# Channel groups with one block's and with three blocks' kernels by turns in block 0, each kind with its own tile of finished rows

## The chip, the cores and the metric

The kernel runs on one core of a Trainium2 chip. The metric is the device time of one execution in microseconds (us). Three runs of the kernel before took 1357.64, 1360.15 and 1365.32 us, median 1360.15.

## The reference

A state-space convolution (S4D) and a feed-forward layer, each behind a layer norm with modulation, on 2048 tokens of 576 channels, all in float32:

```
K  = 2 * Re(sum_n C[d,n] * exp(A[d,n]*dt[d]*l))        # 576 convolution kernels, 2048 long, 128 states
mod = silu(c) @ w_mod                                  # sa, ca, ga, sb, cb, gb
h = layernorm(x) * (1 + ca) + sa
x = x + ga * (causal_conv(h, K) + h * D_skip)          # by FFT of 4096
h = layernorm(x) * (1 + cb) + sb
x = x + gb * (relu(h @ w1) @ w2)                       # 576 -> 4608 -> 576
```

## The kernel before

The tokens are worked through in four blocks of 512. The convolution is done block by block with transforms of its own; block s needs the convolution kernel's rows for block s (called kd[s] in DRAM, in two halves of the channels, p = 0 and 1). The 576 channels are dealt with in 12 groups h of 48; groups 0 to 5 make half p = 0, groups 6 to 11 half p = 1.

A start stage (up to about 222 us) makes the tables W1 and W2 of every group, the rows of block 0, and the convolution of block 0. From then on the feed-forward layer of block b runs as a loop over 36 tiles of the hidden size. Each such step has 14 matmuls into hps (line 1309), ScalarE's relu hh (line 1314), VectorE's remainder hl (line 1315), and 14 matmuls into acc (line 1335) one step later, in TensorE's order. In block 0 a step also splits its weights into a high and a low part (lines 1274 to 1291) and stores the low part for the later blocks.

Between these steps the function `step` takes pieces from a generator of side work, at four places in each step; it stops when the pieces' VectorE estimates or the number of TensorE pieces reach its bounds. The side work of block 0 is `kg.rest`, which makes the kernel rows of blocks 1 to 3, and then the convolution of block 1. A scheduler then sets the order on each engine from its own estimates, so instructions stand somewhat moved against the code.

`kg.rest` goes through a plan of groups. Each entry says for which blocks the group makes rows: `(1, 2, 3)` for groups 0 to 5, a heavy group, and `(1,)` for groups 6 to 11, a light one (blocks 2 and 3 of those follow in block 1's side work). For each group it loads W1 and Z (`load0`) and W2 (`load2`, 1536 KB) on GpSimd's queue, turns W1 on VectorE once for each block (`rot`, lines 464 to 470), and then makes the products on TensorE (line 498) in two halves: 48 channels' matmuls of 48 columns in a heavy group, of 16 in a light one, copied by ScalarE into the tile `ker` (line 508). When half of the channels is done (h % 6 == 5), the rows are stored to kd on SyncE's queue (line 432). Products of one group are mixed with the rotations of the next:

```python
yield from spread(rots(h, W1, W0, Z), prev, len(plan[h]))
prev = products(h, W1, W2)
```

`spread` gives one piece of products after every `len(plan[h])` pieces of rotations, so the products of the group before are spread over 12 pieces of a heavy group's rotations, or over 4 of a light one's. W1 has two buffers, W2 two, the tile `ker` one, and the PSUM tile kps one. The convolution of block 1 begins behind the plan's end: it loads the rows as kt (line 1232, GpSimd's queue) and transforms them (ps_f, line 829).

Of the kernel before, what the change touches and what calls it, by code (L numbers as in the profile page):

```python
# [10 lines left out]
F32 = mybir.dt.float32  # L11
F32R = mybir.dt.float32r
I32 = mybir.dt.int32
AF = mybir.ActivationFunctionType
# [4 lines left out]
P = 128  # L19
L = 2048  # L20
D = 576
# [7 lines left out]
NH = 12  # L29
# [20 lines left out]
class KGen:  # L50
# [10 lines left out]
    def v(self, out, a, b, op):  # L61
        self.tc.keep_in_program_order(self.nc.vector.tensor_tensor(out, a, b, op=op))  # L62
# [373 lines left out]
    def rest(self, psum, plan):  # L436

        nc, k = self.nc, self.k
        v = nc.vector.tensor_tensor
        hs = list(plan)  # L440
        with ExitStack() as ctx:
            pt = k.pool(ctx, f"kr{len(hs)}", side="right")
            most = used = 16 * max(len(b) for b in plan.values())

            d = Kept(k.tc, nc.gpsimd).dma_start

            def load0(h):
                W0 = pt.tile([P, 16, 2, H], F32, tag="W0", bufs=3, name=f"W0_{h}")
                Z = pt.tile([P, 2, 2, H], F32, tag="Z", bufs=3, name=f"Zr_{h}")
                d(out=W0.rearrange("p a r c -> p (a r c)"), in_=k.W1d[h])  # L450
                d(out=Z.rearrange("p i r c -> p (i r c)"), in_=k.Zd[h])
                return W0, Z

            def load2(h):
                W2 = pt.tile([P, 2, 32, H], F32, tag="W2", bufs=2, name=f"W2r_{h}")
                d(out=W2.rearrange("p r b c -> p (r b c)"), in_=k.W2d[h])
                return W2

            def rot(out, X, Z, i):
# [4 lines left out]
                v(T.rearrange(flat), X.rearrange(flat), zi, op=ALU.mult)  # L464
                yield 1.75
                v(out.rearrange(flat), X.rearrange(flat), zr, op=ALU.mult)  # L466
                yield 1.75
                v(out[:, :, 0], out[:, :, 0], T[:, :, 1], op=ALU.subtract)
                yield 0.95
                v(out[:, :, 1], out[:, :, 1], T[:, :, 0], op=ALU.add)  # L470
                yield 0.95

            def rots(h, W1, W0, Z):
                blocks = plan[h]
                a = [W1[:, 16 * i : 16 * i + 16] for i in range(len(blocks))]
                if blocks[0] == 1:
                    yield from rot(a[0], W0, Z, 0)
                    if len(blocks) > 1:
                        yield from rot(a[1], W0, Z, 1)
                        yield from rot(a[2], a[0], Z, 1)  # L480
                else:
                    yield from rot(a[0], W0, Z, 1)
                    yield from rot(a[1], a[0], Z, 0)

            ke = [None]

            def products(h, W1, W2):
                blocks = plan[h]
                na = 16 * len(blocks)
                if h % 6 == 0:  # L490
                    ke[0] = pt.tile([P, most, 72], F32, tag="ke", bufs=1, name=f"ker_{h}")[:, :na]
                for half in range(2):
                    ps = psum.tile([P, 6, na], F32, tag="cps", bufs=1, name="kps")
                    for q in range(6):
                        for dd in range(4):
                            ch = dd * 12 + 6 * half + q
                            for r in range(2):
                                nc.tensor.matmul(  # L498
                                    ps[32 * dd : 32 * dd + 32, q, :],
                                    W2[:, r, :, ch],  # L500
                                    W1[:, :, r, ch],
                                    start=(r == 0),
                                    stop=(r == 1),
                                )
# [3 lines left out]
                    nc.scalar.activation(  # L508
                        ke[0][:, :, q0 : q0 + 6], ps.rearrange("p q a -> p a q"), AF.Copy
                    )  # L510
                    yield None
                if h % 6 == 5:
                    yield -1
                    for i, s in enumerate(blocks):
                        self.store(
                            s, h // 6, ke[0][:, 16 * i : 16 * i + 16].rearrange("p a q -> p (a q)"),
                            nc.sync,
                        )

            nxt = [load0(hs[0])]  # L520
            W2 = load2(hs[0])
            nxt.append(load0(hs[1]))
            yield -1
            prev = iter(())
            for i, h in enumerate(hs):
                W0, Z = nxt.pop(0)
                if i + 2 < len(hs):
                    nxt.append(load0(hs[i + 2]))
                na = 16 * len(plan[h])
                if used + na > most:  # L530
                    all1 = pt.tile([P, most, 2, H], F32, tag="W1", bufs=2, name=f"W1r_{h}")
                    used = 0
                W1 = all1[:, used : used + na]
                used += na
                yield from spread(rots(h, W1, W0, Z), prev, len(plan[h]))
                prev = products(h, W1, W2)
                if i + 1 < len(hs):
                    W2 = load2(hs[i + 1])
            yield from prev


def spread(a, b, n):

    for i, w in enumerate(a):
        yield w
        if i % n == n - 1:
            yield next(b, 0.0)
    yield from b


class Body:
# [3 lines left out]
    def build(self):  # L555
        nc, tc, I = self.nc, self.tc, self.I
        with ExitStack() as ctx:
            dr = ctx.enter_context(tc.tile_pool(name="dram", bufs=1, space=DRAM))
            self.kd = [[dr.tile([P, 16 * 72], F32, name=f"kd_{s}_{p}") for p in range(2)] for s in range(NB)]
            self.W2d = [dr.tile([P, 64 * H], F32, name=f"W2d_{h}") for h in range(NH)]  # L560
            self.W1d = [dr.tile([P, 32 * H], F32, name=f"W1d_{h}") for h in range(NH)]
            self.Zd = [dr.tile([P, 4 * H], F32, name=f"Zd_{h}") for h in range(NH)]
            spec = lambda n, m: [
                [dr.tile([P, 8 * PC], F32, name=f"{n}_{i}_{p}") for p in range(2)] for i in range(m)
            ]
            self.Ud, self.Rd = spec("Ud", 4), spec("Rd", 3)
            self.Kd = self.Rd[:1] + spec("Kd", 3)[1:]
            self.md = {n: dr.tile([1, D], F32, name=f"md_{n}") for n in ("ca", "sa", "gb")}
            self.cst = ctx.enter_context(tc.tile_pool(name="cst", bufs=1))
            self.L1d = [dr.tile([P, 640], F32, name=f"L1d_{f}") for f in range(NF)]  # L570
            self.L2d = [dr.tile([P, D], F32, name=f"L2d_{f}") for f in range(NF)]
            self.consts()
            self.x2, self.xT, self.ended = {}, {}, -1
            self.dsk = self.cst.tile([1, D], F32, name="dsk")
            nc.gpsimd.dma_start(out=self.dsk, in_=I["dsk"].unsqueeze(0))
            self.sm = self.pool(ctx, "sm")
# [168 lines left out]

    def main(self, ctx, kg, hooks):
        nc, tc, I = self.nc, self.tc, self.I
        for n, w in (("sb", 5), ("cb", 5), ("gb", D)):
# [790 lines left out]
```

## Time and profile before

| | us |
|---|---|
| median of 3 runs | 1360.15 (1357.64 to 1365.32) |
| the profiled execution | 1357.89 |
| its span, first to last instruction | 1356.1 |
| TensorE busy | 1239.6 (91%) |
| VectorE busy | 891.6 (66%) |
| ScalarE busy | 494.9 (36%) |
| GpSimd busy | 162.6 (12%) |
| mean granted TensorE clock | 0.944 of full speed |

PE is TensorE, PEld its weight loads, DVE VectorE, ACT ScalarE, POOL GpSimd, SP SyncE. A row of a group has the line, engine, operation, tiles and count, then busy time and the mean of one in ns, then the engine's idle time just ahead and what ended it. A row of the busy times by stretches has, behind the stretch's length, each engine's busy time, then the granted TensorE clock, the mean busy share of the DMA engines and GB/s. "issue" is time in which an engine waited for nothing that the profile shows. The feed-forward loop of block 0 runs from about 222 to 569 us.

### The profile page before, as it was taken

What the parts mean: (1) busy time and instruction counts of PE and PEld (TensorE: products, weight loads), DVE (VectorE), ACT (ScalarE), POOL (GpSimd) and SP (SyncE); (2) the same over time, 40 slices, a digit from 0 to 9 for tenths busy, and PEclk for the clock granted to TensorE, in tenths of its full rate; (3) what the DMA queues carried; (4) which work ended last, traced back from release to release, by engine and by line L of the source; (5) the groups of instructions that cost most, each with busy time, mean ns of one, the idle gap of its engine ahead of it and who ended that gap; (6) DMA issues with size and microseconds to landing.
All of it is one profiled execution on the core that took longest, in us unless ns stands there. A gap on an engine that the chain in (4) does not pass through costs nothing.

```text
span 1356.1 us, 26019 instructions
## 1 busy us (share of the span) xinstructions
PE 1239.6 (91%) x10720; PEld 986.5 (73%) x10720; DVE 891.6 (66%) x1324; ACT 494.9 (36%) x863; POOL 162.6 (12%) x260
## 2 busy tenths in 40 slices
PE   4566777899989999999999999999999999999997
PEld 2345555677767687777777887887888888888885
DVE  5889988999955899678556986367997222111112
ACT  5678423222122432622234225433322353233231
POOL 0657511000010100020000000100000000000000
PEclk9558887999978999999999999999999999999998
DMA  8557973776897877798778995777996557666651
GB/s 267 221 223 291 328 271 130 282 249 248 320 332 277 296 248 269 239 382 311 250 246 327 363 371 158 269 230 245 370 387 194 176 175 228 201 195 195 201 184 53
DMA packets 120843, 345.85 MB, mean 255 GB/s; under 512 B 23916, under 2 KB 24212, under 8 KB 109972
## 3 DMA queue, kind: packets, MB, share of 16 engines
q1 hardware_dynamic: 103828, 226.96, 49.7%
q0 software_dynamic: 16384, 115.85, 22.8%
q8 instruction: 84, 1.38, 0.4%
q10 hardware_dynamic: 512, 1.38, 0.3%
q14 instruction: 35, 0.29, 0.1%
HBM read 262.73 MB, written 81.40 MB: 254 GB/s over the span
## 4 chain that ended last, share of the span: by engine, by line
PE 73%; DVE 15%; DMA 5%; issue 4%; ACT 1%; POOL 1%; SPq 0%; ACTq 0%; DVEq 0%; POOLq 0%
PE acc L1335 29%; PE hps L1309 29%; PE kps L498 4%; PE ps_f L829 4%; PE kps L71 2%; PE ph L71 2%; PE ps_i L1036 2%; DVE T L464 1%; DVE W1r L466 1%; DVE T L62 1%; DMA Ua<-Ud 1%; DVE Y L1015 1%; DMA r<-in_w_dram 1%; DMA kd<-ker 1%; DVE W L62 1%
## 5 line engine op out<-in xcount | busy, mean ns | idle before, releaser
L1309 PE MATMUL hps<-xh,w 128*128 128x512 f32 x1152 | 391.3, 400 | 0.7 <-ACT xh L47 0.7
L1335 PE MATMUL acc<-w,hh 128*128 128x512 f32 x1152 | 371.8, 403 | 7.0 <-ACT hh L1314 7.0
L1315 DVE SCALAR_TENSOR_TENSOR hl<-hps,hh 128x512 fp32r<-128x512 f32 x144 | 99.0, 687 | 322.9 <-ACT hh L1314 321.9
L1335 PEld LDWEIGHTS acc<-w,hh 128*128 128x128 f32 x1152 | 217.6, 190 | 55.1 <-ACT hh L1314 8.3
L1309 PEld LDWEIGHTS hps<-xh,w 128*128 128x128 f32 x1152 | 217.3, 190 | 48.5 <-ACT xh L47 1.3
L1309 PE MATMUL hps<-xl,w 128*128 128x512 f32 x576 | 230.7, 401 | 0.2
L1335 PE MATMUL acc<-w,hl 128*128 128x512 f32 x576 | 224.4, 402 | 3.9 <-DVE hl L1315 3.9
L1314 ACT ACTIVATE hh<-hps 128x512 fp32r<-128x512 f32 x144 | 85.9, 597 | 304.0 <-PE hps L1309 302.3
L1284 ACT ACTIVATE w<-r 128x576 fp32r<-128x576 f32 x141 | 96.6, 685 | 236.7 <-PE acc L1335 207.9
L1335 PEld LDWEIGHTS acc<-w,hl 128*128 128x128 f32 x576 | 109.1, 190 | 28.2 <-DVE hl L1315 5.0
L1309 PEld LDWEIGHTS hps<-xl,w 128*128 128x128 f32 x576 | 108.7, 189 | 24.5 <-DVE xl L47 0.8
L1274 ACT ACTIVATE w<-r 128x640 fp32r<-128x640 f32 x140 | 102.6, 733 | 40.6 <-DMA r<-in_w_dram 40.6
L1309 PE MATMUL hps<-xs,w 128*128 128x512 f32 x288 | 97.1, 410 | 0.3 <-DVE w L1279 0.3
L498 PEld LDWEIGHTS kps<-W1r,W2r 128*32 128x32 f32 x3456 | 66.9, 146 | 32.0 <-issue 23.6
L498 PE MATMUL kps<-W1r,W2r 128*32 128x48 f32 (+2 forms) x3456 | 75.9, 238 | 9.2 <-issue 8.2
L71 PE MATMUL kps<-W,W 128*32 128x16 f32 x2304 | 45.1, 218 | 42.7 <-POOL W L68 28.7
L71 PEld LDWEIGHTS kps<-W,W 128*32 128x32 f32 x2304 | 40.4, 150 | 55.0 <-POOL W L68 30.7
L1015 DVE TENSOR_TENSOR Y<-Y,T 128x1152 f32<-128x1152 f32 x60 | 79.4, 1349 | 0.0
L830 ACT ACTIVATE Z<-ps_f 128x288 f32<-128x288 f32 x120 | 48.7, 408 | 68.8 <-PE ps_f L829 67.6
L1453 POOL DMA_DIRECT2D out_dram<-x x16 | 8.7, 544 | 469.0 <-DVE x L1445 466.3
L1309 PEld LDWEIGHTS hps<-xs,w 128*128 128x128 f32 x288 | 53.3, 188 | 12.4 <-DVE w L1279 0.7
L1335 PE MATMUL acc<-hl,w 128*128 128x512 f32 x144 | 57.3, 398 | 0.0
(230 smaller groups left out, 1567.3 us busy)
## 6 DMA issues: line engine op xcount, KB each, us to landing
r<-in_w_dram SPq DMA_DIRECT2D x144, 320.0 KB, 3.5
r<-in_w_dram SPq DMA_DIRECT2D x144, 288.0 KB, 3.7
w<-L1d SPq DMA_DIRECT2D x108, 320.0 KB
w<-L2d SPq DMA_DIRECT2D x108, 288.0 KB, 2.6
W2r<-W2d POOLq DMA_DIRECT2D x18, 1536.0 KB, 8.3
W2d<-W SPq DMA_DIRECT2D x12, 1536.0 KB, 8.6
Ua<-Ud POOLq DMA_DIRECT2D x15, 1152.0 KB, 9.4
W<-W1d POOLq DMA_DIRECT2D x18, 768.0 KB, 10.7
```

The costliest lines, as they stand in the source:

```text
L62: self.tc.keep_in_program_order(self.nc.vector.tensor_tensor(out, a, b, op=op))
L71: self.tc.keep_in_program_order(self.nc.tensor.matmul(*args, **kw))
L498: nc.tensor.matmul(ps[32 * dd : 32 * dd + 32, q, :], W2[:, r, :, ch], W1[:, :, r, ch], start=(r == 0), stop=(r == 1),)
L829: nc.tensor.matmul(o, fc[:, n2, c, :], src(n2), start=True, stop=True)
L830: ev = nc.scalar.activation(Z[:, n2, c], ps[:, :PC], AF.Copy)
L1015: v(y, y, T, op=op or ALU.add)
L1274: copy(g - 1)(w1[g][:, 0], r1[g], AF.Copy)
L1284: copy(g)(w[:, 0:D], r2[g], AF.Copy)
L1309: nc.tensor.matmul(ps, a, x, start=(i == 0), stop=(i == 13))
L1314: nc.scalar.activation(hh, ps, AF.Relu)
L1315: nc.vector.scalar_tensor_tensor(hl, ps, 0.0, hh, op0=ALU.max, op1=ALU.subtract)
L1335: nc.tensor.matmul(acc[i], a, x, start=(f == 0 and seen[i] == 1), stop=(f == NF - 1 and seen[i] == (3 if i < 4 else 2)),)
```

## The change

The plan of block 0 is no longer in the order of the groups: light and heavy ones come by turns, 6, 0, 7, 1, 8, 2, 9, 3, 10, 4, 5, 11. Each half of the channels now has a tile `ker` of its own (`ke48` for the heavy groups, `ke16` for the light ones), since both are being filled at the same time. The space for it comes from the row of the skip coefficients, which now lies in the tile of the late coefficients gb until those are written.

```diff
-            ke = [None]
+            ke = {}
...
                 if h % 6 == 0:
-                    ke[0] = pt.tile([P, most, 72], F32, tag="ke", bufs=1, name=f"ker_{h}")[:, :na]
+                    ke[h // 6] = pt.tile([P, na, 72], F32, tag=f"ke{na}", bufs=1, name=f"ker_{h}")
...
                     nc.scalar.activation(
-                        ke[0][:, :, q0 : q0 + 6], ps.rearrange("p q a -> p a q"), AF.Copy
+                        ke[h // 6][:, :, q0 : q0 + 6], ps.rearrange("p q a -> p a q"), AF.Copy
                     )
...
-            self.dsk = self.cst.tile([1, D], F32, name="dsk")
+            self.sm = self.pool(ctx, "sm")
+            self.gb = self.sm.tile([P, D], F32, name="m_gb")
+            self.dsk = self.gb[0:1]
             nc.gpsimd.dma_start(out=self.dsk, in_=I["dsk"].unsqueeze(0))
...
             yield from kg.rest(
-                self.cps, {h: (1, 2, 3) if h < 6 else (1,) for h in range(NH)}
+                self.cps, {h: (1, 2, 3) if h < 6 else (1,) for h in (6, 0, 7, 1, 8, 2, 9, 3, 10, 4, 5, 11)}
             )
```

A light group used to take a third of a W1 tile, three groups in a row in one tile; now each light group has a W1 tile for itself.

What this makes of TensorE's order, first in the light groups of the kernel before (kps are the products, hps and acc the feed-forward matmuls; a row of kps counts a matmul once that the trace has twice):

```order
L498 MATMUL kps<-W1r_4614,W2r_4759 32x16 x48
L1335 MATMUL acc_0_3032<-w_4873,hh 128x512 x2
L498 MATMUL kps<-W1r_4614,W2r_4759 32x16 x48
L1335 MATMUL acc_0_3032<-w_4873,hl 128x512
L1335 MATMUL acc_0_3033<-w_4873,hh 128x512 x2
L1335 MATMUL acc_0_3033<-w_4873,hl 128x512
L1335 MATMUL acc_0_3034<-w_4873,hh 128x512 x2
L1335 MATMUL acc_0_3034<-w_4873,hl 128x512
L1335 MATMUL acc_0_3035<-w_4873,hh 128x512 x2
L498 MATMUL kps<-W1r_4614,W2r_4905 32x16 x48
```

Both halves of a light group's products stand two feed-forward matmuls apart, and the next group's follow within a step. In the changed kernel, a heavy group's products (group 2) in the turn of a light one, on TensorE too:

```order
L498 MATMUL kps<-W1r_3746,W2r_3740 32x48
L1311 MATMUL hps<-xh_2820,w_3817 128x512
L1311 MATMUL hps<-xl_2821,w_3817 128x512
L1311 MATMUL hps<-xh_2820,w_3817 128x512 x2
L498 MATMUL kps<-W1r_3746,W2r_3740 32x48 x47
L1311 MATMUL hps<-xl_2821,w_3817 128x512
L1311 MATMUL hps<-xh_2820,w_3817 128x512 x2
L498 MATMUL kps<-W1r_3746,W2r_3740 32x48 x48
L1311 MATMUL hps<-xl_2821,w_3817 128x512
L1311 MATMUL hps<-xh_2820,w_3817 128x512
L1337 MATMUL acc_0_3038<-w_3913,hl 128x512
L498 MATMUL kps<-W1r_3960,W2r_3954 32x16
```

and behind it the light group's products (group 9), now in three pieces within a heavy group's turn:

```order
L1311 MATMUL hps<-xl_2821,w_3919 128x512
L498 MATMUL kps<-W1r_3960,W2r_3954 32x16 x47
L1311 MATMUL hps<-xh_2820,w_3919 128x512 x2
L1311 MATMUL hps<-xl_2821,w_3919 128x512
L498 MATMUL kps<-W1r_3960,W2r_3954 32x16 x24
L1311 MATMUL hps<-xh_2820,w_3919 128x512 x2
L1311 MATMUL hps<-xl_2821,w_3919 128x512
L1311 MATMUL hps<-xh_2820,w_3919 128x512 x2
L1311 MATMUL hps<-xl_2821,w_3919 128x512
L1311 MATMUL hps<-xh_2820,w_3919 128x512
L498 MATMUL kps<-W1r_3960,W2r_3954 32x16 x24
```

The wide products have drawn together and the narrow ones apart. On SyncE's queue the rows of the first half (kd_0, blocks 1 to 3) are stored in the kernel before at this place (L1390 are the stores of the split weights, numbered by step):

```order
L1390 DMA L2d_176<-w_4129 128x576
L1390 DMA L1d_141<-w_4032 128x640
L432 DMA kd_0_59<-ker_3115 64x1152 x2
L432 DMA kd_0_61<-ker_3115 64x1152 x2
L432 DMA kd_0_63<-ker_3115 64x1152 x2
L1254 DMA r_4451<-in_w_dram 128x640
L1258 DMA r_4453<-in_w_dram 128x576
```

and in the changed kernel here, on the same queue:

```order
L1392 DMA L2d_180<-w_4869 128x576
L1392 DMA L1d_145<-w_4772 128x640
L432 DMA kd_0_59<-ker_3239 64x1152 x2
L432 DMA kd_0_61<-ker_3239 64x1152 x2
L432 DMA kd_0_63<-ker_3239 64x1152 x2
L1256 DMA r_5175<-in_w_dram 128x640
L1260 DMA r_5177<-in_w_dram 128x576
L1392 DMA L2d_181<-w_5048 128x576
L1392 DMA L1d_146<-w_4875 128x640
L432 DMA kd_1_60<-ker_3051 64x1152 x2
```

The store of the first half has moved four steps later (behind L1d_145, not L1d_141), and that of block 1's second half follows it one step later; before, it stood behind L1d_148.

More of the change, by code (lines that the diff above doesn't have):

```diff
@@ L515, in products @@
                         self.store(
-                            s, h // 6, ke[0][:, 16 * i : 16 * i + 16].rearrange("p a q -> p (a q)"),
+                            s, h // 6, ke[h // 6][:, 16 * i : 16 * i + 16].rearrange("p a q -> p (a q)"),
                             nc.sync,
@@ L573, in build @@
             self.x2, self.xT, self.ended = {}, {}, -1
-            self.dsk = self.cst.tile([1, D], F32, name="dsk")
+            self.sm = self.pool(ctx, "sm")
+            self.gb = self.sm.tile([P, D], F32, name="m_gb")
+            self.dsk = self.gb[0:1]
             nc.gpsimd.dma_start(out=self.dsk, in_=I["dsk"].unsqueeze(0))
-            self.sm = self.pool(ctx, "sm")
             self.x2p = [self.pool(ctx, "x2a")]
@@ L747, in main @@
         nc, tc, I = self.nc, self.tc, self.I
-        for n, w in (("sb", 5), ("cb", 5), ("gb", D)):
+        self.m["gb"] = self.gb
+        for n, w in (("sb", 5), ("cb", 5)):
             self.m[n] = self.sm.tile([P, w], F32, name=f"m_{n}")
```

## The prediction

> **What bounds the kernel now.** I read the page first, then the busy time by stretches, then TensorE's own timeline in the stretch that the change rebuilds, then the chain of work that ended last.
>
> ```profile
> span 1356.1 us, 26019 instructions
> PE 1239.6 (91%) x10720; PEld 986.5 (73%) x10720; DVE 891.6 (66%) x1324; ACT 494.9 (36%) x863; POOL 162.6 (12%) x260
> q8 instruction: 84, 1.38, 0.4%
> ...
> 1339.01 6.35 PE acc L1335 x28
> ```
>
> TensorE is busy for 91% of the span, and the last row, the end of the chain, is one bare step of the feed-forward part: 28 matmuls, 6.35 us. 144 such steps are 914 us that no order of the rest can shorten. A gain can come only from time in which TensorE idles or runs at a lower clock beside them. So I asked for the stretches of block 0, in which the side work (kernel rows, then the convolution of block 1) runs between the steps.
>
> ```profile
> core 0: us, PE busy (x) PEld busy (x) DVE busy (x) ACT busy (x) POOL busy (x), PEclk, DMA share, GB/s
> 229.00:356.00 127.00, 120.02 (x1520) 94.28 (x1520) 127.00 (x134) 31.20 (x55) 10.65 (x22) 0.97 0.74 271
> 356.00:427.00 71.00, 61.95 (x1303) 49.85 (x1302) 39.28 (x54) 13.06 (x29) 7.99 (x14) 0.86 0.90 324
> 427.00:470.00 43.00, 43.00 (x175) 30.59 (x175) 35.72 (x63) 19.60 (x45) 3.85 (x6) 1.00 0.79 281
> 470.00:545.00 75.00, 72.12 (x311) 57.40 (x309) 72.77 (x101) 20.21 (x34) 3.71 (x7) 1.00 0.73 259
> ```
>
> The first row holds the six channel groups with three blocks' kernels ("heavy"): VectorE has no free moment, TensorE is idle for 7.0 us. The second holds the six groups with one block's kernels ("light"): TensorE is idle for 9.05 us at a clock of 0.86, VectorE is idle for 31.7 us, and the DMA engines are at 0.90. The third and fourth hold the convolution of block 1, bounded first by TensorE, then by VectorE (72.77 of 75). TensorE's timeline shows what happens in the second row (columns: start, duration, engine, line, operation, count, idle time before it and its cause).
>
> ```profile
> 371.21 1.65 PE L498 MATMUL kps<-W1r,W2r 128*32 128x16 f32 x96 [0.86 <-ACT ker L508]
> 372.79 0.50 PE L1309 MATMUL hps<-xs,w 128*128 128x512 f32 x1
> 373.12 0.40 PE L1309 MATMUL hps<-xh,w 128*128 128x512 f32 x1
> 373.45 0.92 PE L498 MATMUL kps<-W1r,W2r 128*32 128x16 f32 x47
> 377.11 0.96 PE L498 MATMUL kps<-W1r,W2r 128*32 128x16 f32 x49 [2.74 <-issue]
> 378.00 0.79 PE L1309 MATMUL hps<-xl,w 128*128 128x512 f32 x1
> 378.59 0.63 PE L1309 MATMUL hps<-xh,w 128*128 128x512 f32 x1
> 379.15 1.40 PE L498 MATMUL kps<-W1r,W2r 128*32 128x16 f32 x77
> 383.31 0.58 PE L498 MATMUL kps<-W1r,W2r 128*32 128x16 f32 x19 [2.75 <-issue]
> ...
> 414.30 0.64 PE L498 MATMUL kps<-W1r,W2r 128*32 128x16 f32 x21 [2.69 <-issue]
> ...
> 419.01 1.22 PE L498 MATMUL kps<-W1r,W2r 128*32 128x16 f32 x67
> ```
>
> Three times TensorE stops for 2.7 us in the middle of a burst of short matmuls, with nothing to wait for that the profile shows. Between the first and the second stop stand 49 + 1 + 1 + 77 = 128 matmuls, each with its weight load: 256 instructions. The page has 84 instruction packets for 2 x 10720 TensorE instructions, 255 each. So I read these stops as the next packet of instructions coming late: 256 instructions were used up in 3.44 us (377.11 to 380.55), and the next ones were there 6.2 us after the first began. The Trainium skill (page "Runtime: NRT & Kernel Launch", section "Instruction fetch mechanics") has the same blocks of 256 instructions, fetched while the one before runs, and calls the cost of crossing "mostly hidden"; the three stops of 2.69 to 2.75 us speak against the last part.
>
> **The change part by part.** First, what goes.
>
> ```profile
> L498 PE MATMUL kps<-W1r,W2r 128*32 128x16 f32 x1152 | 21.1, 213 | 9.1 <-issue 8.2 <-ACT ker L508 0.9
> 376.00:390.00 14.00, 10.14 (x163) 7.97 (x163) 1.54 (x4) 2.29 (x5) 1.58 (x3) 0.52 0.96 355
> 413.00:420.00 7.00, 5.70 (x97) 4.33 (x98) 2.16 (x6) 0.26 (x1) 0.00 (x0) 0.52 1.02 354
> 359.41 11.23 DMA kd<-ker
> ```
>
> (1) The stops, 8.2 us. In the new order a light group's 192 matmuls are spread over the rotations of a heavy one, in pieces of 48 to 94 with feed-forward matmuls between, so 256 instructions of the 16-wide kind never stand close together, but for the last light group. I take all 8.2. (2) The half clock behind the stops: 10.14 + 5.70 = 15.8 us of matmuls ran at 0.52. The short ones hardly feel it (49 in 0.96 us, against 96 in 1.65); they take 0.96 + 1.40 + 0.58 + 0.64 + 1.22 = 4.8 us of it. The other 11.0 us would have taken half: 5.5 at most, I take 5. The Trainium skill (page "TensorE: Matmul & The Clock Gate", section "HAM oscillation — how this bites in real kernels") asks for idle gaps over some 3.4 us before the clock falls; here gaps of 2.7 us were enough. By that rule term 2 would be nothing and the gain 5 us smaller. (3) The wait for the finished rows: with one tile for both kinds, the first light group waits until the heavy rows are stored (11.23 us in the chain), which cost TensorE the 0.9 us on L508. Two tiles end that: 0.9. Together 14 us.
>
> Second, what the heavy stretch does.
>
> ```profile
> L1335 PE MATMUL acc<-w,hh 128*128 128x512 f32 x106 | 32.2, 409 | 7.0 <-ACT hh L1314 7.0
> L498 PE MATMUL kps<-W1r,W2r 128*32 128x48 f32 x1152 | 31.4, 266 | 0.0
> L464 DVE TENSOR_TENSOR T<-W,Zr 128x1536 f32<-128x1536 f32 x14 | 24.5, 1747 | 0.0
> ...
> L464 DVE TENSOR_TENSOR T<-W1r,Zr 128x1536 f32<-128x1536 f32 x6 | 10.5, 1748 | 0.0
> ...
> L1315 DVE SCALAR_TENSOR_TENSOR hl<-hps,hh 128x512 fp32r<-128x512 f32 x14 | 9.5, 681 | 1.2 <-ACT hh L1314 1.2
> ...
> 312.98 2.34 PE L498 MATMUL kps<-W1r,W2r 128*32 128x48 f32 x94
> ```
>
> Here TensorE loses 7.0 us waiting for ScalarE's hh while VectorE is full. L464 opens a rotation and L1315 stands once in a step, so the row counts give VectorE's progress: 20 rotations begun (19.5 done) and 14 steps in 127 us. By the instruction order its 24 rotations still take 17 steps, now at about 1.5 a step throughout, where they came at 1.5 and then at 1. At 100%, 24 rotations and 17.5 steps need some 157 us, to 386 us; TensorE's 17.5 steps (111 us) and its 52.5 us of short matmuls (31.4 + 21.1) need 164 us from 229 us, to 393. Both are nearly full, and out of step with each other: in a light group's turn TensorE has the heavy matmuls (2 x 2.34 = 4.7 us) beside one step, in a heavy group's turn VectorE has three rotations. So the 7.0 us with their half clock (about 1) may go, or 6 us more of the kind may come: -8 to +6, and I take a gain of 2.
>
> Third, what is added. (4) The heavy matmuls now stand closer: 96 and 96 with three to five feed-forward matmuls between. 128 of them take 128 x 2.34/94 = 3.2 us, with those between 3.7 to 3.9. In the heavy stretch none stopped (idle 0.0) at a DMA share of 0.74; at a share near 1 a packet took 6.2 us. The new stretch has the mean of both, some 0.8. Bounds: no stop, or six of 2.4 us with 1.7 us of half clock each (the 5 us of term 2 by three), 25 us. It is nearer to the row without stops; I take 2. (5) The kernel rows of block 1 are now stored behind the second-last group.
>
> ```profile
> 434.31 0.65 PE L829 MATMUL ps_f<-kt,fcK 128*128 128x288 f32 x2
> ...
> kd<-ker SPq DMA_DIRECT2D x12, 288.0 KB, 9.2
> ...
> kt<-kd POOLq DMA_DIRECT2D x6, 576.0 KB, 9.2
> ...
> L1232 POOL DMA_DIRECT2D kt<-kd x6: 1171/1172/1182, 404.5 to 880.9; - x6
> ```
>
> Store (11.2 in the chain), issue (1.2) and load (9.2) are 21.6 us. GpSimd's queue holds the load, and behind it stands only the load of the convolution's remainder R, which in the kernel before waited for the last kernel products too. In the new order 3.8 steps, 24 us, and the last light group's 3.3 us stand between those products and the first transform (434.31 now): 27 us cover 21.6, and I take nothing. Without that cover TensorE, in its order, waits at the transform with all feed-forward matmuls behind it: up to 6 us and 1.7 of half clock. (6) By the order the first transform now stands one feed-forward step later (behind the 22nd first half, not the 21st), and the convolution ends at nearly the same step (34.6, was 34.2). So 0.85 steps fewer lie beside a convolution that VectorE bounds, and TensorE idles for up to 0.85 x 6.35 = 5.4 us there, less what VectorE saves in those steps: 0 to 5.4, I take 3. (7) The skip row in the big tile, its place, and the wider W1 tiles for light groups cost nothing that I can find: the row is read before the late coefficients overwrite it, on queues whose order is the same, and a W1 buffer frees after the products two groups back, as it did for heavy groups.
>
> Sum: 14 + 2 - 2 - 3 = 11 us. The profiled execution took 1357.9 us (span 1356.1 and 1.8 around it), 2.3 below the median of the three runs. I make the sum against it: 1357.9 - 11 = 1347, and let that stand for the median too, since the difference is smaller than what a measurement can tell here, about 0.5% (6.8 us).
>
> **The rivals.** *More goes (0.18).* All waits of the heavy stretch go too and the convolution gives nothing back: 14 + 8 = 22, 1336 us. For it: VectorE's 31.7 idle us are then spread. Against it: TensorE and VectorE are both full at 393 and 386 us. *Given back (0.20).* The stops go, but the convolution is bounded by VectorE, and the rows arrive late: 14 + 2 - 2 - 5.4 - 6 = 3, 1355 us. For it: 72.77 of 75 us busy; the cover of 27 us hangs on steps at full speed. The same no-change comes if the stops have nothing to do with how close the short matmuls stand, but with the traffic of that moment (DMA share 0.96 to 1.02 at each): then 0.9 + 2 - 3 is left, 1358 us. That the page on instruction fetch calls the cost mostly hidden would end there too. *Slower (0.12).* The dense heavy bursts stop for instructions each time: six places, 4.1 us each, 25 us, against the 14 that go and the 3 given back: 1357.9 - 14 + 25 + 3 = 1372 us. It needs packets that take over 3.9 us at the new DMA load, and turns the sign once the six cost more than 1.8 us each on average.
>
> **How the numbers follow.** My forecast of 1347 has 0.50. Faster by over 0.5%: the forecast and the first rival, 0.68. Within 0.5%: 0.20. Slower: 0.12. The range must leave out no more than 2 in 10: 1332 to 1361 holds the forecast, the second rival and most of the first, and leaves out the slow one. The forecast's own range, by its bounds, is 1336 to 1353.
>
> **What would show it.** In the changed kernel's profile between 229 and 427 us: TensorE's idle on L498 with the cause "issue" near zero (8.2 now), a granted clock near 1 where it was 0.86, VectorE's idle time spread, the wait on L508 for the store gone, and the first transform before 434 us with one step more done. Stops of over 2 us inside 48-wide bursts would speak for the slow rival; TensorE waiting at the first transforms for kt, or TensorE idle with VectorE full before the end of the convolution, for the second. If the stops are still there at 16-wide matmuls, my reading of them is wrong.

## The result and the profile after

The changed kernel took 1348.93 us, median of 6 runs (1343.05 to 1351.41), against 1360.05 us for the kernel before in 6 runs on the same chip (1357.64 to 1365.32). The ratio is 0.9908, 95% interval 0.9889 to 0.9927: faster by 0.9%, 2 us from the forecast of 1347. The page of the changed kernel:

```profile
span 1345.6 us, 26013 instructions
PE 1232.3 (92%) x10720; PEld 983.7 (73%) x10720; DVE 892.2 (66%) x1324; ACT 496.4 (37%) x863; POOL 162.4 (12%) x260
```

The span is 10.5 us shorter. More than that is gained ahead of the convolution, which then gives some of it back. First the stretch from the first step to about the first transform, in the kernel before (busy time by stretches, columns as in the prediction):

```profile
222.00:427.00 205.00, 188.38 (x2839) 148.74 (x2840) 171.92 (x195) 48.89 (x90) 20.20 (x37) 0.92 0.78 280
```

And in the changed one:

```profile
222.00:427.00 205.00, 199.46 (x2915) 159.44 (x2915) 179.32 (x214) 54.33 (x101) 19.66 (x36) 0.99 0.83 297
```

TensorE is busy for 11.1 us more of the same 205, at a clock of 0.99 instead of 0.92. VectorE, idle for 33.1 us before, is idle for 25.7. The stretches that answer to those of the prediction:

```profile
229.00:356.00 127.00, 123.50 (x2041) 98.97 (x2040) 120.17 (x125) 32.16 (x59) 13.77 (x26) 1.00 0.85 303
356.00:427.00 71.00, 69.06 (x855) 55.47 (x854) 53.47 (x81) 17.53 (x35) 3.31 (x5) 1.00 0.79 284
427.00:470.00 43.00, 39.25 (x152) 27.57 (x151) 36.61 (x57) 18.47 (x41) 4.39 (x7) 0.96 0.78 285
470.00:545.00 75.00, 70.62 (x299) 56.63 (x298) 72.31 (x110) 19.80 (x32) 3.18 (x6) 0.98 0.68 240
```

The DMA share is evened out: 0.74 and 0.90 before, 0.85 and 0.79 now. The last two rows show the other side: in the convolution TensorE is idle for 3.75 and 4.38 us, where it was idle for 0 and 2.88. What TensorE waited for in the first stretch, in the kernel before (waits from 222 to 427 us: in total, times, longest):

```profile
PE kps L498 <- issue: 8.2, 3, 2.8
PE acc L1335 <- ACT hh L1314: 7.0, 3, 3.1
PE kps L498 <- ACT ker L508: 0.9, 1, 0.9
```

And in the changed one:

```profile
PE kps L498 <- issue: 2.9, 2, 1.9
PE kps L498 <- ACT ker L508: 2.6, 1, 2.6
```

The waits for hh are gone, the stops without a cause fell from three to two shorter ones. The wait for ScalarE's copy (L508) grew from 0.9 to 2.6 us; below it turns out to have another cause. What held up hh, the largest of these waits, is in the kernel before ScalarE's timeline at the longest of the three:

```profile
292.00 0.74 ACT L1274 ACTIVATE w<-r 128x640 fp32r<-128x640 f32 x1 [8.21 <-DMA r<-in_w_dram]
292.64 0.58 ACT L1314 ACTIVATE hh<-hps 128x512 fp32r<-128x512 f32 x1
```

Ahead of each of the three ScalarE had waited for the load of a raw weight r (7.23, 8.01 and 8.21 us), and hh stood behind its copy. The stops that are left, in TensorE's timeline of the changed kernel:

```profile
290.75 1.68 PE L498 MATMUL kps<-W1r,W2r 128*32 128x48 f32 x67
...
294.37 1.40 PE L498 MATMUL kps<-W1r,W2r 128*32 128x16 f32 x81
296.70 0.43 PE L498 MATMUL kps<-W1r,W2r 128*32 128x16 f32 x13 [0.93 <-issue]
...
357.00 0.65 PE L498 MATMUL kps<-W1r,W2r 128*32 128x16 f32 x22
359.58 0.67 PE L498 MATMUL kps<-W1r,W2r 128*32 128x16 f32 x26 [1.94 <-issue]
```

And the convolution, where time was given back. TensorE's waits from 427 to 545 us:

```profile
PE acc L1337 <- ACT hh L1316: 4.2, 1, 4.2
PE ps_f L831 <- ACT Z L832: 3.7, 1, 3.7
```

Both name ScalarE. ScalarE's timeline at the second of them:

```profile
458.97 0.74 ACT L1276 ACTIVATE w<-r 128x640 fp32r<-128x640 f32 x1 [4.15 <-DMA r<-in_w_dram]
459.61 0.39 ACT L832 ACTIVATE Z<-ps_f 128x288 f32<-128x288 f32 x1
```

The pieces of the chain of work that stand at the two waits:

```profile
450.25 0.75 DVE w L1281
451.01 7.94 DMA r<-in_w_dram
...
506.26 0.83 DVE w L1281
507.14 13.03 DMA r<-in_w_dram
```

In both rows of its timeline ScalarE keeps the order of the program: the copy of a raw weight (L1276) waits for its load, and the evacuation that TensorE needs (L832) stands behind it. Each load starts when VectorE has made the remainder of an earlier weight (L1281), which frees the buffer. The two loads of 320 KB took 7.94 and 13.03 us, at a DMA share of 1.01 (busy time by stretches):

```profile
451.00:459.00 8.00, 5.31 (x22) 3.46 (x20) 4.95 (x7) 1.92 (x6) 0.07 (x1) 1.00 1.01 401
507.00:520.00 13.00, 10.13 (x44) 7.68 (x42) 12.48 (x14) 2.60 (x4) 0.00 (x0) 1.00 1.01 393
```

From the first matmul of the first step to its last matmul of all, TensorE took 1123.8 us before and 1114.1 after; by the gaps between its matmul records it was idle for 21.4 and 16.6 us of it. So 4.8 us of the gain are idle time, and the same matmuls took 4.9 us less (1102.4, then 1097.5): I put this down to the clock, which was at half speed for 33.9 us before and 10.3 after. The other 0.8 us lie ahead of the first step.

### The profile page after: what moved, and what is told of

It reads as the page before. It is cut to its first block, busy times and chain, and to the rows that moved or that the text cites. A ratio compares the mean times of both kernels' runs of the same rounds, so it can differ in the third digit from the quotient of the medians.

```text
span 1345.6 us, 26013 instructions
## 1 busy us (share of the span) xinstructions
PE 1232.3 (92%) x10720; PEld 983.7 (73%) x10720; DVE 892.2 (66%) x1324; ACT 496.4 (37%) x863; POOL 162.4 (12%) x260
## 4 chain that ended last, share of the span: by engine, by line
PE 82%; DVE 8%; DMA 4%; issue 3%; ACT 2%; POOL 1%; POOLq 0%; ACTq 0%; SPq 0%; DVEq 0%
PE acc L1337 33%; PE hps L1311 33%; PE kps L498 5%; PE ps_f L831 5%; PE kps L71 2%; PE ps_i L1038 2%; DMA r<-in_w_dram 2%; PE ph L71 1%; DMA Zr<-Zd 1%; DVE T L62 1%; DVE W L62 1%; DVE k L62 1%; PE ps_t L1133 0%; POOL W L68 0%; DMA kt<-kd 0%
## 5 line engine op out<-in xcount | busy, mean ns | idle before, releaser
L1276 ACT ACTIVATE w<-r 128x640 fp32r<-128x640 f32 x140 | 102.5, 732 | 24.7 <-DMA r<-in_w_dram 23.3
L498 PE MATMUL kps<-W1r,W2r 128*32 128x16 f32 (+2 forms) x3456 | 76.4, 238 | 7.3 <-issue 4.7
L832 ACT ACTIVATE Z<-ps_f 128x288 f32<-128x288 f32 x120 | 48.9, 409 | 69.5 <-PE ps_f L831 68.3
```

The costliest lines, as they stand in the source:

```text
L498: nc.tensor.matmul(ps[32 * dd : 32 * dd + 32, q, :], W2[:, r, :, ch], W1[:, :, r, ch], start=(r == 0), stop=(r == 1),)
L832: ev = nc.scalar.activation(Z[:, n2, c], ps[:, :PC], AF.Copy)
L1276: copy(g - 1)(w1[g][:, 0], r1[g], AF.Copy)
```

## The experiments

**What makes TensorE stop: the order, the tiles, the density or the traffic.** Four kernels ran on one chip beside the kernel before (1360.32 us). The first has the change without its order.

```diff
-  ... for h in (6, 0, 7, 1, 8, 2, 9, 3, 10, 4, 5, 11)}
+  ... for h in range(NH)}
```

> The groups in the order of before (six with three blocks' kernels, then six with one block's), with all the rest of the change: a tile of finished rows for each kind, the skip row in the big tile, the wider first tiles. My theory (B: dense 16-wide matmuls use up their instruction packet before the next one is there, under heavy DMA traffic): the three stops of about 2.7 us and the half clock behind them stay, only the wait for the store (0.9 us) goes: 1357 to 1361 us, TensorE's idle time on the kernel products with the cause issue 6 to 9 us. Rival S (the single tile of rows and its store were what held the stretch back, the order does nothing): 1347 to 1351 us, few stops.

Measured: 1357.82 us, ratio 0.9976 (0.9958 to 0.9995; here and below the ratio to the kernel before on the same chip, with its 95% interval). Its short products as a group, 225 to 430 us:

```profile
L498 PE MATMUL kps<-W1r,W2r 128*32 128x16 f32 x1152 | 22.6, 212 | 6.7 <-issue 6.7
```

The stops are there (2.67, 2.96 and 0.68 us among the short matmuls, 1.11 right behind them), the wait for the store is gone, and 5.4 us of waiting for hh are there too. All of the change but its order is worth 0.7 to 5.7 us, and the order is the larger part of the 0.92%. The second kernel has the new order, with a light group's products in one piece.

```diff
-                        if q == 2:
+                        if q == 2 and na > 16:
                             yield None
 ...
-                    yield None
+                    if na > 16 or half:
+                        yield None
```

> The order of the change, but the products of a group with one block's kernels are issued as one piece, where they stood in four, spread over the next group's rotations. Nothing is left out, and each stretch moves the same bytes as in the changed kernel. Theory B: 192 matmuls, 384 instructions with their weight loads, now stand close together, so each of the six such groups crosses one or two packet boundaries too fast; stops of 1 to 2.7 us come back, 5 to 9 of them, with halved clock behind the long ones: 1357 to 1372 us. Rival T (the stops come from the DMA traffic of the moment, however close the matmuls stand): no more stops than in the changed kernel, 1347 to 1351 us.

Measured: 1359.97 us, ratio 0.9999 (0.9982 to 1.0016). The whole gain is gone. Its short products, as a group:

```profile
L498 PE MATMUL kps<-W1r,W2r 128*32 128x16 f32 x1152 | 22.6, 213 | 9.2 <-ACT ker L508 4.7 <-issue 4.5
```

And one of its stops, in TensorE's timeline:

```profile
277.61 0.68 PE L498 MATMUL kps<-W1r,W2r 128*32 128x16 f32 x28 [2.46 <-issue]
```

Three long stops came back (2.46, 1.69, and 2.94 us in the matmuls right behind a burst), not five to nine; TensorE ran 20.8 us at half clock before 427 us, the changed kernel 3.5. So traffic alone (T) does not make them. But joining pieces also changes how `step` paces the side work, so not all 11 us are the stops'. The third and fourth kernels go back to the old order: one leaves out five loads of W2, so that there is less traffic, one leaves out half the short matmuls.

```diff
-                if i + 1 < len(hs):
+                if i + 1 < len(hs) and (len(plan[hs[i + 1]]) > 1 or len(plan[h]) > 1):
                     W2 = load2(hs[i + 1])
```

> The kernel before, in its order, but the last five groups with one block's kernels use the second factor W2 of the first of them again: five loads of 1.5 MB are left out (those rows of the kernel are then of the wrong channels), every matmul stays. The DMA share in the light stretch falls from 0.9 to about 0.5. Theory B (density and traffic together): packets come sooner, the stops shrink to under 1 us or go, no half clock: 1344 to 1350 us. Rival D (density alone, a packet takes some 6 us whatever the traffic): three stops of about 2.7 us as before, 1357 to 1361 us. Rival T (traffic alone): stops gone, as by B; what tells B from T is the run with half the light matmuls.

```diff
-                            for r in range(2):
+                            for r in range(2 if na > 16 else 1):
 ...
-                                    stop=(r == 1),
+                                    stop=(r == 1 or na == 16),
```

> The kernel before, in its order and with all its loads, but in the groups with one block's kernels only the first of the two matmuls that add up to a product is made (576 of 1152 left out, 10.5 us of matmuls by 18.3 ns each): the 16-wide matmuls stand half as dense, under the same traffic. Theories B and D: 256 instructions now take twice as long, the stops go, and the half clock: 1360 - 10.5 - 8.2 - 5 = 1336 us, at most 1340. Rival T: the stops stay at some 2.7 us with the half clock, only the matmuls go: 1348 to 1351 us.

Measured: 1349.34 us, ratio 0.9916 (0.9888 to 0.9945), with less traffic; 1353.76 us, ratio 0.9944 (0.9925 to 0.9963), with half the short matmuls. Less traffic first, the light stretch by busy time:

```profile
356.00:427.00 71.00, 66.78 (x1339) 53.08 (x1337) 47.63 (x74) 17.43 (x40) 4.36 (x7) 1.00 0.65 234
```

Its short products:

```profile
L498 PE MATMUL kps<-W1r,W2r 128*32 128x16 f32 x1152 | 21.9, 211 | 4.2 <-issue 4.2
```

At a mean DMA share of 0.65 for 0.90 two stops remain, of 1.45 and 2.43 us, and the clock stays at 1.00 in that stretch: density alone (D) would have left three of 2.7. Both that remain lie between 370 and 381 us, where the share was still 0.91. From 381 to 427 us it was 0.51, and the short matmuls, as dense as before, stopped once, for 0.35 us. Now half the matmuls, the short products:

```profile
L498 PE MATMUL kps<-W1r,W2r 128*32 128x16 f32 x576 | 10.9, 215 | 10.3 <-ACT ker L508 8.0 <-DMA W2r<-W2d 2.2
```

ScalarE's waits in that kernel from 356 to 427 us:

```profile
ACT w L1284 <- DMA r<-in_w_dram: 11.3, 2, 8.3
ACT ker L508 <- DMA kd<-ker: 5.1, 1, 5.1
```

No stop is left at a DMA share of 0.93 in the same stretch (0.90 in the kernel before). So in this stretch stops of over 1 us came where both met, density and traffic (B). The time fell by 6.6 us and not by 24: the store of the rows, a W2 that has not landed and a raw weight for which ScalarE waits 8.3 us took the place of the stops. As I read it, the light stretch in the old order was nearly as short as its loads allow; no run tests this apart.

What happens at a stop can be read from the trace's records: TensorE's instructions, counted in blocks of 256, and the transfers of instruction packets. "Stop" is the idle time ahead of the next block.

```
kernel               block begun   transfer started    next block begun   transfer to begin   stop
before                 371.47           374.84              377.11              2.27           2.74
before                 377.11           380.95              383.31              2.36           2.75
before                 408.65           412.09              414.30              2.21           2.69
changed                291.30           294.43              296.70              2.27           0.92
changed                352.06           357.14              359.58              2.44           1.94
before, one W2         370.65           372.74              375.01              2.28           1.45
before, one W2         375.01           378.08              380.39              2.31           2.43
```

In the twelve traces of this study 23 such stops of over 0.6 us lie between 225 and 430 us, and in each the next block begins 2.21 to 2.46 us after its packet's transfer has started. What varies is when it starts: 1.3 to 6.3 us after the block before was begun.

**Heavy groups in one piece, and where the turns begin.** The changed kernel with 192 matmuls of 48 columns at a time:

```diff
-                        if q == 2:
+                        if q == 2 and na == 16:
                             yield None
 ...
-                    yield None
+                    if na == 16 or half:
+                        yield None
```

> The changed kernel, but the products of a group with three blocks' kernels are issued as one piece of 192 matmuls of 48 columns, where they stood in two of 96 and two halves; the light ones as in the changed kernel. By the runs so far a packet is there 2.3 us after its transfer starts, and that starts 1 to 4.4 us after the block before it is begun. 128 matmuls of 48 columns take 3.2 us. Theory B: at some of the six heavy groups the next packet is late, by 0 to 2.7 us each: 2 to 5 stops, 3 to 9 us with the clock: 1351 to 1358 us. Rival (only 16-wide matmuls outrun their packets): no more stops than in the changed kernel, 1347 to 1351 us.

Measured: 1361.1 us, ratio 1.0009 (0.9990 to 1.0027).

```profile
L498 PE MATMUL kps<-W1r,W2r 128*32 128x48 f32 x1152 | 29.1, 266 | 0.0
L498 PE MATMUL kps<-W1r,W2r 128*32 128x16 f32 x1152 | 23.7, 212 | 4.9 <-issue 4.1 <-ACT ker L508 0.8
```

In this run the 48-wide matmuls never outran their packets: theory B, that they would, failed here, and its range was too low. They can, though. A later kernel, the one with early loads, in an order with heavy groups as dense as in the changed kernel, has this in TensorE's timeline:

```profile
397.01 2.28 PE L498 MATMUL kps<-W1r,W2r 128*32 128x48 f32 x86
400.30 0.56 PE L498 MATMUL kps<-W1r,W2r 128*32 128x48 f32 x10 [1.00 <-issue]
```

The block that ends there holds 125 matmuls of 48 columns; its next packet's transfer started 2.9 us after the block was begun. The run that undoes the early loads stops at the same place, for 1.16 us. In the run here the short ones stopped TensorE twice (1.31 and 2.76 us). The edit also joined the 32-wide products of block 1: behind 605 us TensorE was idle for 4.9 us, in the changed kernel for none. These are two stops (1.52 and 3.42 us), each at the end of a block of 256 instructions, so dense 32-wide matmuls outran their packets here. And the pace of the side work changed, as above. How much of the 12 us or so is each was not separated. Then the changed kernel with strict turns, a heavy group first:

```diff
-  ... for h in (6, 0, 7, 1, 8, 2, 9, 3, 10, 4, 5, 11)}
+  ... for h in (0, 6, 1, 7, 2, 8, 3, 9, 4, 10, 5, 11)}
```

> The changed kernel with its groups strictly by turns, one with three blocks' kernels first (0, 6, 1, 7, ..., 5, 11). My theory: what counts is that the light group's 16-wide matmuls lie beside a heavy group's rotations, which is so here too; the wait of 2.6 us at the first light group, which comes early in the changed kernel, goes, and the heavy pair 4, 5 is parted: 1344 to 1350 us. Rival: the light group at the very start (VectorE is free for the steps there) is part of the gain: 1350 to 1355 us. The run is also what the next one but two is compared with.

Measured: 1350.66 us, ratio 0.9926 (0.9903 to 0.9950). That is just outside the range of my theory and inside the rival's, but the interval overlaps that of the changed kernel (0.9889 to 0.9927): these runs show no difference by which kind comes first.

**The same stops elsewhere.** Two stores moved out of the setup's last burst of short matmuls.

```diff
-                self.save(self.Ud[s][p], U)
+                self.save(self.Ud[s][p], U, None if s else Kept(self.tc, nc.sync))
```

> The changed kernel, with two transfers of 1152 KB of the first convolution (the stores of its two spectra of the input, which nobody needs before 430 us) put from GpSimd's queue at 161 and 167 us onto SyncE's queue behind the load of the kernel rows at 178 us. Every engine's instructions stay in the same order; nothing is left out. Between 159 and 174 us TensorE runs the last 384 short matmuls of the setup in one piece, at the same density in both kernels, with two stops of 4.93 and 3.77 us in the chain of work that the first convolution waits for. Theory B or T (traffic makes the packets late): the two stops shrink by about 2 us each, and the end comes 3 to 5 us sooner: 1344 to 1346 us. Rival D (a packet takes the same time whatever the traffic): no change, 1347 to 1351 us. If the stores delay the first weights of the feed-forward part behind them, up to 3 us are lost again.

Measured: 1349.09 us, ratio 0.9923 (0.9902 to 0.9944): no change. TensorE's timeline of the changed kernel:

```profile
166.85 2.15 PE L71 MATMUL kps<-W,W 128*32 128x16 f32 x128 [4.93 <-issue]
172.77 1.38 PE L71 MATMUL kps<-W,W 128*32 128x16 f32 x79 [3.77 <-issue]
...
208.28 1.30 PE L1038 MATMUL ps_i<-V,gc 128*128 128x288 f32 x2 [7.46 <-DVE V L47]
```

And of this one:

```profile
165.98 2.16 PE L71 MATMUL kps<-W,W 128*32 128x16 f32 x128 [3.63 <-issue]
170.80 1.43 PE L71 MATMUL kps<-W,W 128*32 128x16 f32 x81 [2.67 <-issue]
...
208.47 0.82 PE L1038 MATMUL ps_i<-V,gc 128*128 128x288 f32 x1 [10.77 <-DVE V L47]
```

At the same density the stops shrank from 8.70 to 6.30 us, as B and T say (the DMA share from 165 to 174 us was 0.49 for 0.96), and the burst ended about 2 us sooner. All of it went into the wait for VectorE's V, which grew by 3.3 us: V came no sooner (208.47 us for 208.28). What VectorE waited for ahead of V, in the changed kernel:

```profile
192.57 2.90 DVE L47 TENSOR_TENSOR K<-Z 128x576 f32<-128x576 f32 x6 [3.95 <-ACT Z L873]
```

And in this one:

```profile
192.77 2.90 DVE L47 TENSOR_TENSOR K<-Z 128x576 f32<-128x576 f32 x6 [6.07 <-DMA Rd<-K]
```

It now waited for the store Rd, which took 10.9 us from its issue at 181.81 us; in the changed kernel it took 6.5. The two moved stores, issued at 179.16 and 179.64 us, ran beside it (DMA share from 178 to 193 us: 1.05 for 0.88). So by the trace the moved stores took back at their new place what the shorter stops had given; no run tests that apart.

**What the convolution gave back.** The kernel with strict turns, with raw weights loaded one step earlier.

```diff
-            r1[g] = ff.tile([P, 5, P], F32, tag="r1", bufs=2, name="r1")
+            r1[g] = ff.tile([P, 5, P], F32, tag="r1", bufs=3, name="r1")
 ...
-                if g + 3 < n:
-                    load_r1(g + 3)
-                if g + 2 < n:
-                    load_r2(g + 2)
+                if g + 4 < n:
+                    load_r1(g + 4)
+                if g + 3 < n:
+                    load_r2(g + 3)
 ...
-                    all1 = pt.tile([P, most, 2, H], F32, tag="W1", bufs=2, name=f"W1r_{h}")
+                W1 = pt.tile([P, na, 2, H], F32, tag=f"W1{na}", bufs=nb, name=f"W1r_{h}")
```

> The kernel with turns from the heavy group, with raw feed-forward weights loaded one step earlier (three buffers for each of the two raw tiles instead of two); the room comes from first-factor tiles of their own size for light groups, one less buffer of the factors in the second block, and the last output tile sharing a buffer. Theory G (what the change gave back in the convolution of block 1 is weight loads that land late under a full DMA: ScalarE waits for them, with the evacuations that TensorE needs queued behind): the two stalls of about 4 us in the convolution and the half clock behind them go: 5 to 9 us faster than the run with turns from the heavy group. Rival V (VectorE bounds the convolution anyway, the stalls come back at another place): within 2 us of that run.

Measured: 1344.11 us, ratio 0.9887 (0.9866 to 0.9908), 6.6 us below the run with strict turns on the same chip, as theory G said. Since other edits make the room, one run undoes the early loads alone, beside a second run of the same kernel.

```diff
-            r1[g] = ff.tile([P, 5, P], F32, tag="r1", bufs=3, name="r1")
+            r1[g] = ff.tile([P, 5, P], F32, tag="r1", bufs=2, name="r1")
 ...
-                    load_r1(g + 4)
+                    load_r1(g + 3)
```

> The kernel with raw weights loaded one step earlier, with that alone undone: two raw buffers and the loads where they stood; the first-factor tiles of their own size and the other room-making edits stay. Theory G (the earlier loads are what gained 6.5 us): as the run with turns from the heavy group, 1349 to 1353 us, with two stalls of 2.5 to 4.5 us in the convolution of block 1. Rival (the tiles of their own size gained it, by letting rotations start sooner or later): 1343 to 1346 us.

> The kernel with raw weights loaded one step earlier once more, beside the run that undoes it, on the same chip. Theory G: 5 to 8 us below that run, 1342 to 1346 us.

Measured: 1353.05 us, ratio 0.9934 (0.9917 to 0.9951), with the late loads; 1343.07 us, ratio 0.9864 (0.9850 to 0.9879), with the early ones. TensorE's waits from 427 to 545 us with the late loads:

```profile
PE ps_f L827 <- ACT Z L828: 4.6, 1, 4.6
PE acc L1333 <- ACT hh L1312: 4.1, 1, 4.1
```

ScalarE's longest for a raw weight in the same stretch:

```profile
ACT w L1282 <- DMA r<-in_w_dram: 21.1, 4, 10.1
```

With the early loads (the second run of it) ScalarE has no wait for r there, and TensorE this one of over 0.3 us:

```profile
PE acc L1333 <- ACT hh L1312: 2.8, 1, 2.8
```

The intervals of these two runs do not overlap, and two stalls of over 4 us have become one of 2.8. That one has another cause: ScalarE now waits for stores of the split weights (L1d, 12.6 us in all), where it waited for loads. TensorE's idle time from 427 to 605 us is 6.8 us in both runs with early loads, 9.9 and 11.7 us in the two without (5.3 in the kernel before). So most of the give-back was late weight loads (G). Not all of the 10 us between the last two runs is that: their profiled executions lie 16.7 us apart, and about half of it lies ahead of the convolution. The version with turns and early loads is 1.1 and 1.4% under the kernel before in its two runs, the changed kernel 0.9%.

## Why the prediction was right, point by point

**(1) The stops, 8.2 us: right in kind, too large.** They fell from 8.2 to 2.9 us, so 5.3 went. The step that failed is "never stand close together": the block that ends at 296.70 us holds 48-wide matmuls of a heavy group and 81 short ones right behind them. And the block need not be that dense: the one that ends at 359.58 lasted 5.6 us, but its next packet's transfer started only 5.1 us after it was begun and the packet was there after 7.5 us, not the 6.2 that I had read. Late packets as the cause are shown by the table of blocks; that density and traffic both count, by the runs with dense light groups, with less traffic and with half the matmuls.

**(2) The half clock, 5 us: right.** The 20.5 us at half speed behind the stops are gone. By an estimate from this trace, their 24 feed-forward matmuls took 5.5 us more than 24 of the mean length at full clock. The 4.9 us of the whole run are a net figure: the convolution has 6.8 us at half speed that were not there before. The Trainium skill (page "TensorE: Matmul & The Clock Gate", section "HAM oscillation — how this bites in real kernels"), whose gaps of over 3.4 us would have made this term nothing, does not fit: no gap of the kernel before in the light stretch was over 2.75 us.

**(3) The store, 0.9 us: right for the wait** (it is gone), and the run without the new order is 0.7 to 5.7 us faster, other causes included. But L508 has 2.6 us by another way: at the first light group ScalarE's copy stood behind a raw weight that came late. I had not looked at those loads.

**The heavy stretch, a gain of 2 us (-8 to +6): the sign was right, the size too low and the mechanism wrong.** The 7.0 us of waiting for hh all went, at the edge of the range. I had put them on a full VectorE, out of step with TensorE. The trace shows ScalarE held up by raw weights that land late, as in (6); how far VectorE delays those loads, by freeing their buffers late, is not separated. That the order takes them away is borne out by the run without it (5.4 us of them) and the one with strict turns (1.7 us). Why it does stays open: in the changed kernel ScalarE waits no less for raw weights from 229 to 356 us (37 us in all, 28 before), but TensorE only once, at L508.

**(4) Dense heavy bursts, a loss of 2: nothing was lost.** No 48-wide matmul of the changed kernel waited for a packet, and none in pieces of 192. The slow rival's mechanism exists, but is rare: in three of the twelve traces a block of 48-wide matmuls ended in a stop of 0.6 us or more (0.60 with dense light groups, 1.00 with early loads, 1.16 with these undone).

**(5) The rows, 0: right.** The first transform came at 424.99 us (434.31 before), without a wait:

```profile
424.99 0.65 PE L831 MATMUL ps_f<-kt,fcK 128*128 128x288 f32 x2
```

**(6) The convolution, a loss of 3 (0 to 5.4): the sign was right, the size too low, the mechanism wrong.** TensorE's idle time from 427 to 605 us rose from 5.3 to 11.1 us, 5.8, just over the bound. I put it on VectorE with fewer steps beside it. The two stalls are raw weights that land late under a full DMA and hold ScalarE up, and with earlier loads most of it went, with VectorE's work unchanged. VectorE enters at one place in the chain: its L1281 frees the buffer, and so sets when such a load starts. ScalarE had waited for these loads before as well, without TensorE noticing (its waits from 427 to 545 us in the kernel before):

```profile
ACT w L1274 <- DMA r<-in_w_dram: 16.6, 4, 8.0
ACT w L1284 <- DMA r<-in_w_dram: 8.9, 2, 7.0
```

And in the changed kernel:

```profile
ACT w L1286 <- DMA r<-in_w_dram: 28.5, 6, 10.0
ACT w L1276 <- DMA r<-in_w_dram: 9.7, 6, 4.2
```

**(7) Nothing: right for the time, wrong on the W1 tiles.** No wait on the skip row shows. For a W1 tile VectorE waits until the products have read it (its waits from 222 to 430 us in the changed kernel):

```profile
DVE W1r L466 <- PE kps L498: 6.8, 4, 2.4
```

There are none in the kernel before, and these are all of VectorE's idle time from 229 to 356 us. TensorE's waits from 222 to 427 us, above, show none that follows from them.

Ahead of the convolution the sum was 14 + 2 - 2 = 14 us. Measured there: the first transform came 9.3 us sooner, with 35 more feed-forward matmuls done (602 for 567), which at 6.35 us for 28 are 7.9 us. That is 17 us, of which 0.8 lie ahead of the first step. Behind it -3 was said, and what is left of the 10.5 is about -7. The total, 11 forecast and 10.5 in the profiled runs, is so close by luck: the two misses cancel. The forecast's own range does not follow from its bounds either: 14 - 6 - 5.4 = 2.6 us is 1355, not 1353, before (4) and (5) are counted.

## What to carry to other kernels

A stop of TensorE with no cause, in the middle of short matmuls, is worth counting in blocks of 256 instructions: if it stands at a block's end, spread those matmuls among long ones, or thin out the transfers beside them. When TensorE waits for an engine, look at what that engine waited for: here the waits that looked like ScalarE's were loads of raw weights. Before a stretch is made faster, look at the loads of the next one in the same way: one more buffer for each of two raw weight tiles, with the loads one step earlier, gained 6.6 and 10 us where the change itself had gained 11. And when transfers are moved out of one stretch, look at what they will stand beside in the other: the two moved stores gained nothing.

## What was not expected of the hardware

**The clock is set window by window.** In the clock rows of all twelve traces changes come only at multiples of 3.41 us. For each such window between 225 and 600 us I took TensorE's idle time and the clock of the window behind it:

```
clock   idle in the window   windows   next window at half clock
full    under 1.4 us           1179               1
full    1.4 to 1.9 us            27              13
full    over 1.9 us              29              29
half    under 0.5 us             42               0
half    over 0.5 us              18              17
```

So what halves the clock is not a gap's length but how much of it falls into one window. The 2.67 us stop of the run with two tiles (362.77 to 365.43) put 1.17 and 1.50 us into two windows and cost no clock; the 2.96 us stop of the same run put 1.61 into one and cost 6.8 us at half speed. The windows do not start with the kernel's work (a border lies at 375.8 us in the kernel before, and at 377.6 us in the run with two tiles, 1.8 us and not a whole window off), so the same stop costs its clock in one run and not in another. The Trainium skill (page "TensorE: Matmul & The Clock Gate", section "What's actually happening") has a free-running window of about 3.4 us, which agrees; it names an idle window as what brings the low clock, which does not: 1.9 idle us of 3.41 were enough each time.

**The last part of an instruction packet's way hardly varies.** From the start of its transfer to the first instruction of its block it took 2.2 to 2.5 us in all 23 stops, and 2.5 and 2.9 us at the two stops of the setup's last burst in the changed kernel. The Trainium skill (page "Runtime: NRT & Kernel Launch", section "Instruction fetch mechanics") calls the crossing mostly hidden. Both are in the kernel before: the block begun at 399.21 us was used up in 2.71 us without a stop, as its next packet's transfer started 0.24 us after it; the three in the table started 3.4 to 3.8 us after, and none was hidden.
